# Issuing the store of the first 256 columns of the last token tile from SyncE after the branch join, not from ScalarE inside each branch

## The chip, the cores and the metric

The kernel runs on one core of one Trainium2 chip. The metric is the device time of one execution in microseconds (us); the time before is the median of three runs. A profile of one further execution gives the instruction records, the DMA records and the granted clock.

## What is computed

A transformer-like block on 2048 tokens of width 448, all in float32: an S4 convolution branch and a SwiGLU feed-forward branch, each behind a layer norm that is modulated by a conditioning vector `c`. The reference, cut to its core:

```python
mod = (_silu(c) @ w_mod).reshape(c.shape[0], 6, 1, -1)
sa, ca, ga, sb, cb, gb = (mod[:, k] for k in range(6))
h = _layernorm(x) * (1 + ca) + sa
x = x + ga * _A_ref(h, A_re, A_im, B_re, B_im, C_re, C_im, log_dt, Dskip)   # convolution over the 2048 tokens
h = _layernorm(x) * (1 + cb) + sb
x = x + gb * ((_silu(h @ w_gate) * (h @ w_up)) @ w_down)                     # 448 -> 1792 -> 448
return x
```

## The kernel before

The tokens are cut into 16 tiles of 128 rows (`NT`), a tile being a [128, 448] float32 buffer `xs[i]` in on-chip memory (224 KB), and the tiles into six blocks of 2, 2, 3, 3, 3, 3 (`BLOCKS`, `TILES`). For each block, `ffn` runs over 14 slices of the hidden width (`NF`): `gate_up` (matmuls of line 754, then SiLU on ScalarE, product on VectorE, and a split into a high and a low part) and `down` (matmuls of line 804), while the other engines prepare the next block.

Two versions of this stand in the program, one behind the other: a run-time flag, computed near the start, decides between `small_path` and `general_path` (`tc.If(rv > 0)` and `cond.Else()`, lines 1042 to 1050). The profiled inputs take the first version. At its end every engine jumps over the second version to the join; the profile gives these jumps as COMPARE_BRANCH of line 1042. Behind the join stand only the last stores (lines 1051 to 1053) and the program's closing sequence (the waits for the DMAs and a barrier of all engines, line 1087 in the profile).

The last block (tiles 13, 14 and 15) ends in `finish`. Its matmuls (line 832) leave four sums in four banks: tile 13, tile 14, columns 0 to 255 of tile 15, and columns 256 to 447 of tile 15. VectorE adds each to `xs[i]` (line 843), in this order. Behind the third addition ScalarE issues the store of its 256 columns (line 845), in each version of the program. The stores of tile 13, tile 14 and the last 192 columns of tile 15 are issued by SyncE behind the join (line 1053). SyncE's and ScalarE's DMAs go to two queues, q1 and q10 in the profile; both are served by the core's 16 DMA engines, which also carry the instruction queues q8 and q14. Each engine executes its instructions in order, and so a DMA issue that takes long, or waits, holds back the issues behind it on the same engine. The schedule is written by hand; nothing reorders it.

Of the kernel before, what the change touches and what calls it, by code (L numbers as in the profile page):

```python
# [16 lines left out]
L, D, N, F = 2048, 448, 256, 1792  # L17
NT = L // 128
# [38 lines left out]
def tile_kernel(ctx, tc, x, a_re, a_im, b_re, b_im, c_re, c_im, log_dt,  # L57
                wd, wgate_up, states, groups, vecs, dft, idft, out):
    nc = tc.nc
    sy, ve, sc, po, pe = nc.sync, nc.vector, nc.scalar, nc.gpsimd, nc.tensor  # L60
# [10 lines left out]
    def bank():  # L71
        t = psg.tile([128, 512], F32, name="bank")
        return t

    xs = {}
# [121 lines left out]
    def make_h(h, i, part=None, ca=ca1, sh=sa):  # L197
        m, rs = n1.of[i][0:2]
        if part != 1:
            ve.scalar_tensor_tensor(h, xs[i], m, ca, op0=OP.subtract, op1=OP.mult)  # L200
        if part != 0:
            ve.scalar_tensor_tensor(h, h, rs, sh, op0=OP.mult, op1=OP.add)  # L202
# [527 lines left out]
    def run_blocks(pools, stages, first=None):  # L730
        work, hid = pools.work, pools.hid
        def ffn(ts, fresh, last, todo):
# [89 lines left out]
            def finish():  # L822
                o = [bank(), bank(), CV, DN[0]]
                A, B = slice(0, 256), slice(256, D)
                part = [(0, slice(0, D)), (1, slice(0, D)), (m, A), (m, B)]

                def sums(f, ks):
                    (hi, lo), (wh, wl) = pp[f], wp[f]
                    for k in ks:
                        q, c = part[k]  # L830
                        for z, (u, v) in enumerate(((hi, wh), (hi, wl), (lo, wh))):
                            pe.matmul(o[k][:, c], u[:, q * 128:(q + 1) * 128], v[:, c],
                                      start=f == NF - 2 and z == 0, stop=f == NF - 1 and z == 2)

                sums(NF - 2, (0, 1))
                sums(NF - 1, (0,))
                sums(NF - 2, (2,))
                sums(NF - 1, (1, 2))
                sums(NF - 2, (3,))
                sums(NF - 1, (3,))  # L840
                for k, (q, c) in enumerate(part):
                    i = ts[q]
                    ve.tensor_tensor(xs[i][:, c], o[k][:, c], xs[i][:, c], op=OP.add)  # L843
                    if k == 2:
                        sc.dma_start(out[i * 128:(i + 1) * 128, c], xs[i][:, c])

            for f in range(NF):
                gate_up(f, f + 2 if fresh and f + 2 < NF else None)
# [12 lines left out]
            if last:  # L861
                return finish()
# [144 lines left out]
    def general_path(pools, y):  # L1007
        work = pools.work
        hs = {}

        def s0(i):
            h = h_of(i)
            make_h(h, i)
            t = v0_of(i)
            sy.dma_start(t, y[i * 128:(i + 1) * 128, :])
            po.tensor_tensor(h, h, gd, op=OP.mult)
            po.tensor_tensor(t, t, g0, op=OP.mult)
            hs[i] = h, t

        def s1(i):  # L1020
            h, t = hs.pop(i)
            ve.tensor_tensor(xs[i], h, xs[i], op=OP.add)
            ve.tensor_tensor(xs[i], xs[i], t, op=OP.add)

        def first(i):
            s0(i)
            s1(i)

        return lambda b: (s0, s1), first
# [16 lines left out]
    with cond.Else():  # L1046
        y = general_conv()
        with ExitStack() as es:
            pools = Pools(es)
            run_blocks(pools, *general_path(pools, y))  # L1050
    for i in TILES[-1]:
        c = slice(256 if i + 1 == NT else 0, D)
        sy.dma_start(out[i * 128:(i + 1) * 128, c], xs[i][:, c])


_INS = ["A_u", "A_A_re", "A_A_im", "A_B_re", "A_B_im", "A_C_re", "A_C_im", "A_log_dt", "B_w_down"]
# [29 lines left out]
def build(nc, aps, out):  # L1086
    with tile.TileContext(nc) as tc:
        a = dict(aps)
        tile_kernel(tc, a["A_u"].rearrange("b l d -> (b l) d"), *[a[n] for n in _INS[1:] + ["B_w_gate_up", "A_states", "w_mod_groups", "c_log_dt", "dft", "idft"]],
                    out.rearrange("b l d -> (b l) d"))  # L1090
# [20 lines left out]
```

## Time and profile before

| What | us |
|---|---|
| Median of three runs | 471.81 (471.29 to 472.66) |
| The profiled execution, its device time | 471.9 |
| The profiled execution, span from first to last instruction | 469.8 |
| Last matmul of `finish` starts | 464.7 |
| Last addition of `finish` (line 843) starts | 465.0 |

The granted TensorE clock was 0.999 over the span. A row of the timeline gives the start, the duration, the engine (with a q for its sequencer, which issues DMAs), the line, the operation, and the tiles written and read. A row on one source line gives the number of instructions, then the shortest, the median and the longest duration in ns, and when the first and the last start. "DMA to landing" is the time from the start of an issue to the last part of its data being reported as written. A row on a DMA queue gives its packets, their megabytes, and the time that they took as a share of all 16 DMA engines in that stretch.

### The profile page before, as it was taken

The page shows a single profiled execution, that of the slowest core. Times are in us where ns is not written, and L with a number is a line of the kernel's source. Part 1 is how long each engine was busy: PE and PEld are TensorE (multiplying, and loading weights), DVE is VectorE, ACT ScalarE, POOL GpSimd, SP SyncE. Part 2 cuts the span into 40 slices and gives each one's busy share as a digit, 9 for nine tenths or more (in the row PEclk, how much of TensorE's full clock was granted, in tenths as well). Part 3 has the DMA queues.
Part 4 walks back from the last instruction along what each step waited for, and adds up shares of the span by engine and source line. Part 5 has one row for each costly group of instructions (what it writes and reads, how often), then busy time and mean ns, then how long its engine had stood idle before and what let it go on. Part 6 is the DMA issues. An engine that isn't in the chain of part 4 may idle for free.

```text
span 469.8 us, 7027 instructions
## 1 busy us (share of the span) xinstructions
PE 460.1 (98%) x2735; PEld 438.2 (93%) x2735; DVE 282.6 (60%) x540; ACT 160.1 (34%) x359; POOL 61.6 (13%) x88
## 2 busy tenths in 40 slices
PE   6999999999999999999999999999999999999995
PEld 3669999999999999999999999999999999999995
DVE  4888999778866447573754766464666543222124
ACT  5879666512343222233212223311223222221111
POOL 1122001000000223200022410004141000000000
PEclk9999999999999999999999999999999999999999
DMA  8976653110003000111300011130000112000001
GB/s 303 407 254 179 204 183 102 58 42 2 2 0 100 0 1 0 46 46 46 117 2 0 2 45 46 45 119 1 1 22 24 46 45 80 22 1 1 1 0 65
DMA packets 18779, 31.24 MB, mean 67 GB/s; under 512 B 2608, under 2 KB 13488, under 8 KB 18736
## 3 DMA queue, kind: packets, MB, share of 16 engines
q1 hardware_dynamic: 18096, 30.53, 19.2%
q8 instruction: 23, 0.38, 0.4%
q10 hardware_dynamic: 640, 0.18, 0.2%
q14 instruction: 20, 0.16, 0.1%
HBM read 24.61 MB, written 6.03 MB: 65 GB/s over the span
## 4 chain that ended last, share of the span: by engine, by line
PE 95%; DMA 3%; DVE 1%; SPq 0%; ACT 0%; issue 0%; DVEq 0%
PE bank L754 61%; PE dn L804 28%; DMA wm<-in_w_mod_groups_dram 2%; DMA vec<-in_c_log_dt_dram 1%; PE dn L476 1%; PE bank L256 1%; PE bank L977 1%; PE cv L976 1%; PE cv L978 1%; PE bank L227 0%; SPq L300 0%; DVE x L843 0%; PE bank L394 0%; PE cv L989 0%; PE bank L266 0%; PE bank L269 0%
## 5 line engine op out<-in xcount | busy, mean ns | idle before, releaser
L754 PE MATMUL bank<-hhi,gu 128*128 128x384 f32 (+1 forms) x1176 | 208.9, 317 | 0.2 <-issue 0.2
L754 PEld LDWEIGHTS bank<-hhi,gu 128*128 128x128 f32 x1176 | 189.4, 188 | 3.1 <-issue 1.1
L754 PE MATMUL bank<-hlo,gu 128*128 128x384 f32 (+1 forms) x672 | 130.8, 317 | 0.0
L754 PEld LDWEIGHTS bank<-hlo,gu 128*128 128x128 f32 x672 | 109.1, 188 | 0.2
L784 DVE TENSOR_TENSOR bank<-raw,bank 128x384 f32<-128x384 f32 (+1 forms) x69 | 36.8, 534 | 117.8 <-PE bank L754 115.5
L791 ACT CAST phi<-bank 128x384 fp32r<-128x384 f32 (+1 forms) x83 | 36.8, 444 | 138.9 <-DVE bank L784 138.8
L769 ACT ACTIVATE raw<-bank 128x384 f32<-128x384 f32 (+1 forms) x70 | 32.9, 470 | 119.3 <-PE bank L754 103.7
L792 DVE TENSOR_TENSOR plo<-bank,phi 128x384 fp32r<-128x384 f32 (+1 forms) x83 | 42.5, 511 | 37.6 <-ACT phi L791 37.6
L804 PE MATMUL dn<-wdh,phi 128*128 128x448 f32 x218 | 57.2, 364 | 0.0
L804 PE MATMUL dn<-wdh,plo 128*128 128x448 f32 x218 | 57.1, 362 | 0.0
L804 PE MATMUL dn<-wdl,phi 128*128 128x448 f32 x218 | 56.9, 362 | 0.0
L804 PEld LDWEIGHTS dn<-wdh,plo 128*128 128x128 f32 x218 | 40.9, 187 | 2.7
L804 PEld LDWEIGHTS dn<-wdl,phi 128*128 128x128 f32 x218 | 40.9, 187 | 2.7
L804 PEld LDWEIGHTS dn<-wdh,phi 128*128 128x128 f32 x218 | 38.6, 188 | 1.2
L185 POOL TENSOR_SCALAR rsb<-mvb 128x1 f32<-128x1 f32 (+2 forms) x13 | 4.6, 354 | 142.0 <-DVE mvb L157 142.0
L125 DVE TENSOR_TENSOR gu<-raw,gu 128x1024 fp32r<-128x1024 f32 x14 | 17.1, 1219 | 1.2 <-ACT gu L123 1.2
L185 POOL TENSOR_SCALAR rsa<-mva 128x3 f32<-128x3 f32 (+1 forms) x6 | 2.3, 381 | 98.7 <-DVE mva L157 96.4
L951 POOL TENSOR_TENSOR m<-m,gm 128x448 f32<-128x448 f32 x9 | 10.4, 1155 | 20.8 <-DVE m L202 17.1
L965 DVE TENSOR_TENSOR vl<-m,vh 128x448 fp32r<-128x448 f32 x12 | 9.1, 757 | 6.7 <-ACT vh L964 6.1
L122 ACT CAST gu<-raw 128x768 fp32r<-128x768 f32 x14 | 11.7, 833 | 0.0
L970 POOL TENSOR_TENSOR m<-m,gd 128x448 f32<-128x448 f32 x9 | 11.5, 1280 | 0.0
L215 ACT ACTIVATE raw<-raw,rsb 128x64 f32<-128x64 f32 x14 | 4.8, 345 | 18.9 <-DVE raw L212 9.7
(243 smaller groups left out, 410.2 us busy)
## 6 DMA issues: line engine op xcount, KB each, us to landing
raw<-in_B_w_gate_up_dram SPq DMA_DIRECT2D x14, 512.0 KB, 3.8
rawd<-in_B_w_down_dram SPq DMA_DIRECT2D x16, 224.0 KB, 3.9
x<-in_A_u_dram SPq DMA_DIRECT2D x12, 224.0 KB, 2.9
out_dram<-x SPq DMA_DIRECT2D x11, 224.0 KB, 2.0
xd<-raw SPq DMA_DIRECT2D x9, 256.0 KB, 2.0
raw<-xd SPq DMA_DIRECT2D x36, 64.0 KB, 1.9
wm<-in_w_mod_groups_dram SPq DMA_DIRECT2D x5, 448.0 KB, 8.2
wm<-in_w_mod_groups_dram SPq DMA_DIRECT2D x5, 336.0 KB, 8.2
```

Source lines behind the costliest of these rows:

```text
L122: sc.copy(wgu[j][:, :, 0:3, :], w[:, :, 0:3, :])
L125: ve.tensor_tensor(wgu[j][:, :, 3:7, :], w[:, :, ::-1, :], f32(wgu[j][:, :, 0:4, :][:, :, ::-1, :]), op=OP.subtract)
L185: po.tensor_scalar(rs[:, 0:n], self.mv[:, 0:n, 1], EPS, None, op0=OP.add)
L754: pe.matmul(ps[s][:, 0:n], w[:, s, a], (hlo if lo else hhi)[:, k, first_col(n):first_col(n) + n], start=first and q == 0, stop=end and q = ...
L769: sc.activation(p[:, 0:n], ps[0][:, 0:n], AF.Silu)
L784: ve.tensor_tensor(ps[1][:, 0:n], p[:, 0:n], ps[1][:, 0:n], op=OP.mult)
L791: sc.copy(hi[:, 0:n], ps[1][:, 0:n])
L792: ve.tensor_tensor(lo[:, 0:n], ps[1][:, 0:n], f32(hi[:, 0:n]), op=OP.subtract)
L804: pe.matmul(dn[q][:, 0:D], u[:, cs], v, start=f == 0 and z == 0, stop=f == (NF - 3 if last else NF - 1) and z == 2)
L951: (ve if on_v else po).tensor_tensor(v, h, g, op=OP.mult)
L965: ve.tensor_tensor(vl, v0, f32(vh), op=OP.subtract)
L970: (ve if on_v else po).tensor_tensor(h, h, gd, op=OP.mult)
```

## The change

The issue of ScalarE inside `finish` goes, in both versions. The loop behind the join splits tile 15 into its two column ranges, so that SyncE issues four stores there in place of three. The diff:

```diff
@@ -841,8 +841,6 @@
                 for k, (q, c) in enumerate(part):
                     i = ts[q]
                     ve.tensor_tensor(xs[i][:, c], o[k][:, c], xs[i][:, c], op=OP.add)
-                    if k == 2:
-                        sc.dma_start(out[i * 128:(i + 1) * 128, c], xs[i][:, c])
@@ -1048,9 +1046,10 @@
     for i in TILES[-1]:
-        c = slice(256 if i + 1 == NT else 0, D)
-        sy.dma_start(out[i * 128:(i + 1) * 128, c], xs[i][:, c])
+        for c in (slice(0, 256), slice(256, D)) if i + 1 == NT else (slice(0, D),):
+            sy.dma_start(out[i * 128:(i + 1) * 128, c], xs[i][:, c])
```

SyncE's instructions at the end of the program, before (-) and with the change (+). `x_73`, `x_74` and `x_75` are the buffers of tiles 13, 14 and 15; what is waited for stands in brackets, DMAHW being the semaphore of an earlier DMA:

```order
 L811 DMA rawd_83<-in_B_w_down_dram 128x448 [waits DMAHW6_49,DVE_49]
-L1042 UNCONDITIONAL_BRANCH
-L1053 DMA out_dram<-x_73 128x448 [waits DMAHW2_49,DVE_49]
-L1053 DMA out_dram<-x_74 128x448 [waits DMAHW3_49,DVE_49]
-L1053 DMA out_dram<-x_75 128x192 [waits DMAHW4_49,DVE_49]
-L1087 UNCONDITIONAL_BRANCH
+L1040 UNCONDITIONAL_BRANCH
+L1052 DMA out_dram<-x_73 128x448 [waits DMAHW1_49,DVE_49]
+L1052 DMA out_dram<-x_74 128x448 [waits DMAHW2_49,DVE_49]
+L1052 DMA out_dram<-x_75 128x256 [waits DMAHW3_49,DVE_49]
+L1052 DMA out_dram<-x_75 128x192 [waits DMAHW4_49,DVE_49]
+L1086 UNCONDITIONAL_BRANCH
```

The store of 256 columns now stands between the store of tile 14 and the store of the last 192 columns, in SyncE's order and on SyncE's queue.

ScalarE's instructions at the end of the program (the lines of the changed kernel are two lower from here on):

```order
 L769 ACTIVATE raw<-bank 128x384 [waits PE_49,Activation_49]
 L778 CAST phi<-bank 128x128 [waits DVE_49] x3
-L845 DMA out_dram<-x_75 128x256 [waits DVE_49]
-L1042 UNCONDITIONAL_BRANCH
-L1087 UNCONDITIONAL_BRANCH
+L1040 UNCONDITIONAL_BRANCH
+L1086 UNCONDITIONAL_BRANCH
```

ScalarE's jump to the join now stands right behind its last cast. The instructions of TensorE, VectorE and GpSimd are the same as before, in the same order.

## The prediction

> **What bounds the kernel now.** I read the page first, then the timeline of the end, then the rows of the store lines, then the DMA queues in short stretches.
>
> ```profile
> span 469.8 us, 7027 instructions
> PE 460.1 (98%) x2735; PEld 438.2 (93%) x2735; DVE 282.6 (60%) x540; ACT 160.1 (34%) x359; POOL 61.6 (13%) x88
> PE 95%; DMA 3%; DVE 1%; SPq 0%; ACT 0%; issue 0%; DVEq 0%
> ```
>
> TensorE is busy 98% of the span and 95% of the chain of waits. Its instructions do not change. What can move is the end, when TensorE is done:
>
> ```profile
> 462.87 0.27 ACT L778 CAST phi<-bank 128x128 fp32r<-128x128 f32 x1 [0.69 <-DVE bank L777]
> ...
> 463.57 1.15 DVE L843 TENSOR_TENSOR x<-bank,x 128x448 f32<-128x448 f32 x2
> ...
> 464.21 2.80 SPq L1053 DMA_DIRECT2D out_dram<-x  x3
> ...
> 464.63 0.42 DVE L843 TENSOR_TENSOR x<-cv,x 128x256 f32<-128x256 f32 x1
> ...
> 465.03 0.36 DVE L843 TENSOR_TENSOR x<-dn,x 128x192 f32<-128x192 f32 x1
> 465.08 0.36 ACTq L845 DMA_DIRECT2D out_dram<-x  x1
> ```
>
> All results are in on-chip memory at 465.39 (465.03 + 0.36), yet the span ends at 469.8. These 4.4 us are stores and closing sequence. The second and the third of SyncE's stores and ScalarE's, one by one:
>
> ```profile
> L1053 SPq DMA_DIRECT2D out_dram<-x x1: 1249/1249/1249, 464.7 to 464.7; - x1
> ...
> DMA to landing us min/median/max: 3.7/3.7/3.7
> ...
> L1053 SPq DMA_DIRECT2D out_dram<-x x1: 931/931/931, 466.1 to 466.1; - x1
> ...
> DMA to landing us min/median/max: 2.6/2.6/2.6
> ...
> L845 ACTq DMA_DIRECT2D out_dram<-x x1: 363/363/363, 465.1 to 465.1; - x1
> ...
> DMA to landing us min/median/max: 2.8/2.8/2.8
> ```
>
> Tile 14's issue takes 1.25 us, that of the last 192 columns (not begun until tile 14's is over, though its data were ready at 465.4) 0.93. The landings are at 464.75 + 3.7 = 468.4, 466.1 + 2.6 = 468.7 and, for ScalarE's, 465.08 + 2.8 = 467.9. The store of the last 192 columns lands last, and the end follows 469.8 - 468.7 = 1.1 us behind it. What the change is worth is how far that landing moves.
>
> A store issue need not take so long. Three stores with 0.84 us between them, in an earlier block:
>
> ```profile
> L867 SPq DMA_DIRECT2D out_dram<-x x3: 333/356/357, 306.8 to 309.2; - x3
> ...
> DMA to landing us min/median/max: 1.9/2.0/2.2
> ```
>
> So the two issues at the end are held up by 0.9 and 0.6 us. The queues show by what:
>
> ```profile
> q8 instruction: 1, 0.02, 6.6%
> ...
> q10 hardware_dynamic: 126, 0.11, 45.2%
> q14 instruction: 2, 0.02, 10.1%
> q1 hardware_dynamic: 10, 0.01, 6.9%
> ...
> q8 instruction: 1, 0.02, 5.5%
> ```
>
> The first row is for 464 to 465: one instruction packet, which starts at 464.6 and takes 6.6% of 16 engines for 1 us, that is 1.05 us of one engine. The middle three are for 465.75 to 466.5: SyncE's queue (q1) moves 10 packets, left-overs of tile 13, while ScalarE's (q10) moves 126. Tile 14's data are not yet moving, since SyncE's issue hangs until 466.0. ScalarE's store passed it. In the same stretch two more instruction packets lie on single engines. The last row (467.25 to 468.3) is a further one, 0.92 us. My reading: while one DMA engine carries an instruction packet, SyncE's queue takes one more DMA and holds the next issue until that engine is free. Two rows from earlier speak for it:
>
> ```profile
> L86 SPq DMA_DIRECT2D x<-in_A_u_dram x1: 1393/1393/1393, 92.9 to 92.9; - x1
> ...
> q8 instruction: 1, 0.02, 125.8%
> ```
>
> The load at 92.9, issued behind others, took 1.39 us; the instruction packet beside it starts in the stretch 92.90 to 92.95 and takes 125.8% of 16 engines for 0.05 us, 1.0 us.
>
> Where the packets come from: each engine jumps to the join and must have new instructions.
>
> ```profile
> L1042 PEldq COMPARE_BRANCH x1: 3430/3430/3430, 463.7 to 463.7; - x1
> L1042 DVEq COMPARE_BRANCH x1: 51/51/51, 465.0 to 465.0; - x1
> L1042 ACTq COMPARE_BRANCH x1: 43/43/43, 465.5 to 465.5; - x1
> ...
> L1087 ACTq DRAIN x1: 81/81/81, 468.1 to 468.1; - x1
> L1087 DVEq DRAIN x1: 59/59/59, 468.3 to 468.3; - x1
> L1087 SPq DRAIN x1: 7/7/7, 469.0 to 469.0; - x1
> ```
>
> TensorE's jump takes 3.43 us; VectorE is back 3.3 us after its jump, ScalarE 2.6. The Trainium skill, "Runtime: NRT & Kernel Launch", section "Instruction fetch mechanics", says that a taken branch whose target is outside the current window forces a DMA fetch before execution goes on. The trace agrees, with packets about 1 us behind the jumps; the page's 16 KiB blocks fit q8 (one packet, 0.02 MB) but not q14, whose two packets share 0.02 MB.
>
> **The change part by part.**
>
> *Removed.* ScalarE's issue (0.36 us) and a store that never lands last: nothing on the path. ScalarE's jump moves from 465.5 to right behind its last cast, 463.1 (462.87 + 0.27). Its instruction packet moves as much, to about 464, ahead of all stores: one of the two q14 packets leaves the stretch in which the stores run. Between nothing and the 0.6 us by which the third issue is held up now may be saved by it.
>
> *Unchanged.* Tile 13 at 464.21; tile 14 from 464.75 to 466.0, since TensorE's jump and its packet stay. TensorE's and VectorE's code is the same.
>
> *Added.* A fourth issue on SyncE, at 466.1, where that of the last 192 columns stands now. Bounds: 0.33 us (shortest row of line 867) to 1.25 us (tile 14's). I take 0.93, what the issue at this instant, behind the same two stores and beside VectorE's packet, takes now: it is the nearest row. It ends at 467.0. Behind it, with 0.1 us between issues (466.1 - 466.0), the last 192 columns start at 467.1 in place of 466.1. Their own issue then takes 0.36 (line 867) in place of 0.93, since the packets of VectorE and ScalarE are past, and ends at 467.5 in place of 467.0: 0.5 us later. The landing came 468.7 - 467.0 = 1.7 us behind the end of the issue; undisturbed it is 2.0 - 0.36 = 1.6. So 469.1 to 469.2, **0.4 to 0.5 us later**. TensorE's second packet (0.92 us of one engine, from 467.8) can hold a sixteenth of these data:
>
> ```profile
> 464.50:465.00 0.50, 0.49 (x5) 0.32 (x3) 0.50 (x2) 0.00 (x0) 0.00 (x0) 1.00 0.13 33
> 465.00:465.25 0.25, 0.00 (x0) 0.00 (x0) 0.25 (x2) 0.00 (x0) 0.00 (x0) 1.00 0.65 244
> ```
>
> The last two columns are the DMA share and GB/s. Tile 13's data begin about 465.05, 0.5 us behind the end of its issue (464.21 + 0.34). So the last columns' data would begin at 468.0, and the held engine is free at 468.7. This is up to 0.2 us more, and I count it in the range.
>
> *Elsewhere.* Both versions lose one ScalarE instruction; no wait, buffer or order before 463 changes. The cost is nothing, and no cover is needed for it.
>
> Sum: 0 + 0 + 0.45. Against the profiled execution 471.9 + 0.45 = 472.35; against the median, which lies 0.1 lower, 472.3. The bounds: with both new issues short, -0.7 (below); with both held, +1.9 (below).
>
> **The rivals.**
>
> *A. Only the bytes count.* The four stores are the same 672 KB on the same 16 engines, whoever issues them, if no issue is held up. At 466.5 there remain 448 KB (224 + 128 + 96), 0.46 MB.
>
> ```profile
> 91.91 0.92 SPq L86 DMA_DIRECT2D rawd<-in_A_u_dram  x2
> ...
> 466.50:466.75 0.25, 0.00 (x0) 0.00 (x0) 0.00 (x0) 0.00 (x0) 0.00 (x0) 1.00 0.81 307
> ...
> 467.25:467.50 0.25, 0.00 (x0) 0.00 (x0) 0.00 (x0) 0.00 (x0) 0.00 (x0) 1.00 0.18 63
> ```
>
> Two issues that follow each other freely take 0.46 us each (first row), so the last would end at 466.1 + 0.92 = 467.0, as now. At the 307 GB/s of the second row the bytes take 1.5 us, until 468.0, with 0.4 us to the landing (now the last data move at 468.3 and land at 468.7): 468.4, 0.3 us earlier than now, so 471.5. For it: with ScalarE's packet gone, the issue at 466.1 may be short. Against it: the engines stand almost idle in the third row because the next issue was late, so issues do count today. The floor of this case is VectorE's return at 468.3: the last drain of SyncE, at 469.0, can come forward to that at most, 0.7 us, 471.1. The Trainium skill, "DMA: Bandwidth & Descriptors", section "Issuing engines are not separate DMA queues", speaks for this rival: all issuers' DMAs run on the same 16 engines, and issuing on several saves only sequencer time. The trace differs in one point: ScalarE's store flowed while SyncE's was held.
>
> *B. Slower beyond doubt: a third hold-up.* The issue of the 256 columns takes tile 14's 1.25 us, until 467.35, and the next one, from 467.45, is still at work when TensorE's second packet starts (467.8). It is then held until that packet ends, 467.8 + 0.92 = 468.7, plus the 0.3 us that tile 14's issue stays behind its packet (464.6 + 1.05 = 465.7, end 466.0): 469.0. Landing 1.6 behind, 470.6, against 468.7: +1.9 us, and +1.6 if it is released at the packet's very end. I put it between, at 473.5. It decides where the fourth issue has not ended by 467.8. Against it: line 867's issues into an idle queue were short each time, and from 467.25 to 467.5 the queues are nearly empty.
>
> *C. Something outside the end*, by the shifted ScalarE code: no row speaks for it; TensorE is busy 98% up to there whatever the other engines fetch.
>
> **How the numbers follow.** About 0.3% (1.4 us) is what a measurement of this kernel can tell from no change; the three runs spread over 1.4 us. Forecast (+0.45): 0.48, of which 0.05 would be measured over +0.3%. Rival A: 0.29, of which 0.03 under -0.3%. Rival B: 0.17, of which 0.12 over +0.3%. C: 0.06, half each way. Faster 0.03 + 0.03 = 0.06; slower 0.05 + 0.12 + 0.03 = 0.20; within 0.74. The forecast's own range is 471.8 to 472.8; from A's 471.5 less 0.4 of spread up to the lower part of B gives 471.1 to 473.4.
>
> **What would show it.** In the changed profile: tile 14's issue still about 1.25 us; the issue of the 256 columns at 466.1 near 0.9 (A: near 0.4; B: over 1.2); the last issue at 467.1, near 0.4; the last landing at 469.1; ScalarE's drain at about 466 in place of 468.1, and TensorE's jump still 3.4 us. A time outside 471.1 to 473.4 with the same code on TensorE would mean that the end isn't what moved, and the reading of the hold-ups falls if tile 14's issue is short although the packet at 464.6 is there.

## The result, and the profile after

The changed kernel takes 472.9 us in the median of 22 runs (471.24 to 473.8), the kernel before 471.6 beside it: a ratio of 1.0026, 95% interval 1.0019 to 1.0033, or 1.2 us slower (0.9 to 1.6). That is within the 0.3% that the prediction called no change (the upper end of the interval, 0.33%, just passes it), but clear of zero. The times are not spread around one value: three of the 22 runs lie between 471.24 and 471.45, the other nineteen from 472.38 on.

The end of the profiled execution (span 471.9 us), from its timeline:

```profile
463.07 0.27 ACT L778 CAST phi<-bank 128x128 fp32r<-128x128 f32 x1 [0.69 <-DVE bank L777]
...
464.42 3.18 SPq L1052 DMA_DIRECT2D out_dram<-x  x4
...
465.23 0.36 DVE L843 TENSOR_TENSOR x<-dn,x 128x192 f32<-128x192 f32 x1
```

All four stores are SyncE's now. This execution comes to its end 0.2 us later than that of the kernel before (first store at 464.42, before 464.21); I count from the first store's issue where I compare. The last three issues, from the rows of the store line:

```profile
L1052 SPq DMA_DIRECT2D out_dram<-x x1: 1432/1432/1432, 464.9 to 464.9; - x1
...
L1052 SPq DMA_DIRECT2D out_dram<-x x1: 631/631/631, 466.5 to 466.5; - x1
...
DMA to landing us min/median/max: 2.0/2.0/2.0
...
L1052 SPq DMA_DIRECT2D out_dram<-x x1: 400/400/400, 467.2 to 467.2; - x1
...
DMA to landing us min/median/max: 3.6/3.6/3.6
```

Tile 14's issue is held as before, the issue of the 256 columns hardly (0.63), the last one is free (0.40). But the last store lands 3.6 us behind its issue, at 470.8, where the store before it needed 2.0. SyncE waits for it:

```profile
SPq L1087 <- DMA out_dram<-x: 1.5, 3, 0.8
...
SPq L1086 <- DMA out_dram<-x: 3.0, 3, 2.3
```

The first row is the kernel before, the second the changed one; each gives the total in us, the number of waits and the longest. One wait in the closing sequence takes 2.3 us; the longest of this kind was 0.8 before. The DMA queues show what happens, in three stretches (468.20 to 468.25, 468.6 to 469.6, and 469.6 to 470.4):

```profile
q8 instruction: 1, 0.02, 179.4%
q1 hardware_dynamic: 22, 0.02, 102.0%
...
DMA packets 1, 0.01 MB, mean 8 GB/s; under 512 B 0, under 2 KB 0, under 8 KB 0
...
DMA packets 9, 0.01 MB, mean 8 GB/s; under 512 B 1, under 2 KB 9, under 8 KB 9
...
q1 hardware_dynamic: 9, 0.01, 5.8%
```

At 468.2 an instruction packet on q8 begins in the middle of the last store's data. The profile doesn't name the owner of a packet; I take this one for TensorE's second, since it comes 0.6 us behind TensorE's return at 467.6 and since q8's packets move with TensorE's jump in f2. Its size: 179.4% of 16 engines for 0.05 us is 1.44 us of one engine, until 469.66. For a whole microsecond no data of the store move (the one packet of the second stretch is another instruction packet). Then nine packets of SyncE's queue follow, eight of a row each and one small one: a sixteenth of 128 rows and its report, what one DMA engine has to do for this store. So 15 of 16 parts were done before 468.6, and the one behind the instruction packet made the kernel wait.

ScalarE is back at 465.7, and TensorE's jump took 3.62 us. ScalarE's earlier jump did not clear the stretch of the stores, though. From 465.9 to 466.8 there are again two packets on q14, as there were before:

```profile
q14 instruction: 2, 0.02, 5.8%
```

One of them starts 0.6 us behind ScalarE's return, as TensorE's second does behind TensorE's; that it is a second packet of ScalarE's is my reading, since the profile doesn't name its owner.

### The profile page after: what moved, and what is told of

Same layout as the page of the kernel before. It is cut to its first block, busy times and chain, and to the rows that moved or that the text cites. A ratio compares the mean times of both kernels' runs of the same rounds, so it can differ in the third digit from the quotient of the medians.

```text
span 471.9 us, 7028 instructions
## 1 busy us (share of the span) xinstructions
PE 461.5 (98%) x2735; PEld 439.4 (93%) x2735; DVE 282.7 (60%) x540; ACT 159.8 (34%) x359; POOL 61.5 (13%) x88
## 4 chain that ended last, share of the span: by engine, by line
PE 94%; DMA 3%; DVE 1%; SPq 0%; ACT 0%; issue 0%; DVEq 0%
PE bank L754 60%; PE dn L804 28%; DMA wm<-in_w_mod_groups_dram 2%; DMA vec<-in_c_log_dt_dram 1%; PE dn L476 1%; PE bank L256 1%; PE bank L975 1%; PE cv L976 1%; PE cv L974 1%; PE bank L227 0%; DVE x L843 0%; PE cv L987 0%; PE bank L394 0%; PE bank L266 0%; SPq L300 0%; PE bank L269 0%
```

## The experiments

**The packet theory**: what is lost is the last store's share on the one DMA engine that carries TensorE's second instruction packet. It is lost when that engine's rows of the store are not past when the packet starts. **The issue theory**, the rival: four issues one behind the other on SyncE are slower than three on SyncE and one on ScalarE, whatever the packets. Ratios are against the kernel before, run beside each.

**e1: four matmuls more on TensorE behind the last.**

```diff
                 sums(NF - 1, (3,))
+                for _ in range(4):
+                    pe.matmul(DN[1][:, 0:D], pp[NF - 1][0][:, 0:128], wp[NF - 1][0], start=True, stop=True)
```

> The changed kernel with four more 448-column matmuls on TensorE behind the last of finish, into a bank that nobody reads: nothing else changes, and TensorE's jump to the join comes about 0.8 us later. Packet theory (the loss is the share of the last store on the one DMA engine that carries TensorE's second instruction packet): that packet starts at about 469.0 in place of 468.2, behind the last store's data; the last landing is at 468.8 to 469.0 in place of 470.8, and the kernel gets FASTER than the changed one by some 1 us in the median (0 to +0.4 us against before) although it does more work. Issue theory (the loss is that SyncE issues four stores one behind the other): no gain, +1.2 us against before as the changed kernel, or more.

Measured: 473.9 us, 1.0038 (1.0025 to 1.0051), +1.8 us. The jump did not move as intended.

```profile
L1042 PEldq COMPARE_BRANCH x1: 3546/3546/3546, 464.1 to 464.1; - x1
...
q8 instruction: 1, 0.02, 180.2%
...
DMA packets 9, 0.01 MB, mean 6 GB/s; under 512 B 1, under 2 KB 9, under 8 KB 9
```

The jump is at 464.1, in an execution whose first store is 0.1 us later than in the changed kernel's, so it came about 0.05 us later and not 0.8. The second packet starts between 468.30 and 468.35, and the same nine packets are late (stretch 469.6 to 470.6). The jump starts ahead of the matmuls that stand before it: the four new ones run from 465.13 to 466.12. So matmuls that wait for nothing do not hold TensorE's sequencer back here; f2 shows a wait that does. The run does not tell the theories apart; it repeats the loss.

**e2: five stores.**

```diff
-        for c in (slice(0, 256), slice(256, D)) if i + 1 == NT else (slice(0, D),):
+        for c in (slice(0, 256), slice(256, 352), slice(352, D)) if i + 1 == NT else (slice(0, D),):
```

> The changed kernel with the last 192 columns stored in two parts of 96, five issues on SyncE in place of four. Packet theory: the rows that are held leave when the packet ends (469.7), whether in one store or two: last landing 470.8 to 471.1, +1.3 to +1.6 us against before. Issue theory: every issue on SyncE costs 0.5 to 0.7 us at the end, so +1.8 to +2.0 us against before.

Measured: 474.35 us, 1.0047 (1.0034 to 1.006), +2.2 us with an interval of 1.6 to 2.8: over what the packet theory expected, and nearer to the issue theory's 1.8 to 2.0.

```profile
L1052 SPq DMA_DIRECT2D out_dram<-x x5: 338/441/1628, 464.6 to 468.0; - x5
...
q8 instruction: 1, 0.02, 169.4%
...
DMA packets 18, 0.01 MB, mean 9 GB/s; under 512 B 18, under 2 KB 18, under 8 KB 18
```

In the profile the packet theory's picture stands: twice nine packets, of both small stores, come behind the instruction packet (470.0 to 470.7). But tile 14's issue was held 1.63 us here, so everything behind it is later, and all five runs lie above 473.6: by their times, no execution got its data past the packet. By its time alone the run is inconclusive.

**e3: tile 15 in one store by SyncE.**

```diff
-        for c in (slice(0, 256), slice(256, D)) if i + 1 == NT else (slice(0, D),):
+        for c in (slice(0, D),):
```

> The changed kernel with tile 15 stored whole, three issues on SyncE and none on ScalarE. The last store is issued at about 466.5 in place of 467.2, its data move from 467.5 to 468.2. Packet theory: nearly all of them are past when TensorE's second packet starts at 468.2; last landing about 468.7, 0 to +0.3 us against before; where a few rows are caught in the profile they land at 470 to 470.8. Issue theory: one issue less than the changed kernel, one fewer step of 0.5 to 0.7 us: +0.5 to +0.7 us against before.

Measured: 472.07 us, 1.0008 (0.9999 to 1.0017), +0.4 us with an interval of 0 to 0.8. The twelve runs lie from 471.34 to 473.53. The last store begins earlier, at 465.9, 2.1 us behind the first (in the changed kernel 2.8); the packet starts in 467.80 to 467.95 beside the last few rows and reports:

```profile
L1052 SPq DMA_DIRECT2D out_dram<-x x3: 337/728/1473, 463.8 to 465.9; - x3
...
q8 instruction: 1, 0.02, 36.6%
q1 hardware_dynamic: 15, 0.01, 13.5%
```

Nothing was late in this execution (span 469.5). By the time both theories remain, since the measured interval covers what either expected.

**e4: the two parts of tile 15 exchanged.** SyncE stores the 256 columns, ScalarE the last 192, inside each version.

```diff
+                    if k == 3:
+                        sc.dma_start(out[i * 128:(i + 1) * 128, c], xs[i][:, c])
...
-        for c in (slice(0, 256), slice(256, D)) if i + 1 == NT else (slice(0, D),):
+        for c in (slice(0, 256) if i + 1 == NT else slice(0, D),):
```

> ScalarE issues the store of the last 192 columns inside each version (behind the fourth addition), SyncE those of tile 13, tile 14 and the 256 columns. Packet theory: ScalarE's store is past by 467, SyncE's third is issued at 466.1 to 466.5 and moves before 468; last landing at 468.5 to 468.7, -0.3 to +0.1 us against before. Issue theory: three issues on SyncE as before: 0.

Measured: 472.13 us, 1.0000 (0.9992 to 1.0009), as both expected. Its profile shows how a packet holds an issue:

```profile
L1054 SPq DMA_DIRECT2D out_dram<-x x3: 337/338/1326, 465.1 to 466.1; - x3
...
q8 instruction: 1, 0.02, 110.2%
```

TensorE's first packet came late in this execution, at 466.10 (the stretch 466.10 to 466.15), 1.0 us behind the first store's issue, where it was 0.4 before. Tile 14's issue, past by then, took 0.34 us, and the next one, which began at 466.1, was held 1.33. One point of the expectation failed: ScalarE's store was not past by 467, but was issued at 466.3 and landed 3.1 us later. The run was the slowest of its eleven (472.78).

**f1: the changed kernel once more, as the control.**

> The changed kernel once more, as the control for the two kernels beside it. Both theories: +0.9 to +1.6 us against before. Packet theory: a profile in which the 16th part of the last landing comes some 2 us behind the 15th, or, if this execution is one of the few that the first series had near 471.3 us, with it.

Measured: 473.24 us, 1.0024 (1.0007 to 1.004), +1.1 us as expected, with a wide interval (0.3 to 1.9). Five of its twelve runs lie from 471.37 to 472.03, the other seven from 473.16 to 475.48. The profiled one was the quickest, 471.37, span 469.5:

```profile
L1052 SPq DMA_DIRECT2D out_dram<-x x4: 338/438/1517, 464.0 to 466.7; - x4
...
DMA to landing us min/median/max: 1.7/2.6/3.3
...
q8 instruction: 1, 0.02, 114.4%
q1 hardware_dynamic: 12, 0.00, 33.8%
...
SPq L1086 <- DMA out_dram<-x: 1.0, 3, 0.5
```

This is the run that decides most, since the program is the same. Four issues on SyncE, tile 14's held 1.52 us, the last at 466.7: 2.7 us behind the first, as in the slower profile (2.8). The second packet starts at 467.96, when only a few rows and reports of the store are left. The last store lands 1.7 us behind its issue, at 468.4, 4.4 behind the first issue; in the slower profile it is 6.4, and in the kernel before 4.5 (468.7 - 464.2). Four issues alone thus cost nothing here. What differs is 0.1 us in the last issue (2.7 against 2.8 behind the first) and 0.2 us in the packet (4.0 against 3.8).

That the store's data are still moving when the packet starts is not enough. In the kernel before, too, it starts among them, at 467.85 (the rows are for 467.8 to 467.9), and nothing is late:

```profile
q8 instruction: 1, 0.02, 57.9%
q1 hardware_dynamic: 29, 0.02, 55.6%
```

The traces have the rows of the last store by their 768 bytes. The packet starts 0.12 us behind the first of them in the changed kernel's profile and 0.20 in e1's, where eight rows were held, and 0.33 to 0.34 in the kernel before and in the control, where none was. One such row takes 0.036 us in the median, so an engine with nothing else to do has its eight past in about 0.3 us (an estimate, 8 times 0.036). This fits the theory; it rests on four profiles, and none names the engine that a packet or a row is on.

**f2: TensorE's jump waits for the last addition.**

```diff
                     ve.tensor_tensor(xs[i][:, c], o[k][:, c], xs[i][:, c], op=OP.add)
+                pe.matmul(DN[1][:, 0:8], xs[ts[m]][:, 256:384], xs[ts[m]][:, 440:D], start=True, stop=True)
```

> The changed kernel with one 8-column matmul on TensorE that reads what VectorE's last addition writes, so that TensorE's sequencer waits for that addition before it jumps (four matmuls without a wait left the jump nearly where it was, since the sequencer runs ahead of the array). The jump comes at about 465.7 in place of 463.9, its first instruction packet at 466.6 in place of 464.8, the second at about 470 in place of 468.2. Packet theory: tile 14's issue is not held (0.34 to 0.45 us in place of 1.43), the last issue begins before 466.6, its data are past long before the second packet, and the last landing is at 468.0 to 468.6; the end is then set by TensorE's return at 469.3, so 0 to +0.5 us against before, some 1 us FASTER than the control. Issue theory: four issues on SyncE as in the control, +0.9 to +1.6 us.

Measured: 472.58 us, 1.0016 (1.0008 to 1.0025): +0.8 us, over the 0 to +0.5 of the packet theory, quicker than the control by less than I expected, and the intervals overlap. By its time the run does not tell the theories apart.

```profile
L1041 PEldq COMPARE_BRANCH x1: 4410/4410/4410, 465.2 to 465.2; - x1
...
463.97 1.86 SPq L1053 DMA_DIRECT2D out_dram<-x  x4
...
L1053 SPq DMA_DIRECT2D out_dram<-x x4: 338/370/407, 464.0 to 465.4; - x4
...
q8 instruction: 1, 0.02, 231.8%
...
DMA to landing us min/median/max: 4.1/4.1/4.1
```

With the jump moved from 463.9 to 465.2, no issue is held: four of them take 1.86 us with the waits between. That half was as expected. The other half was not: the first packet, at 466.18, now lies in the data of the two last stores and takes 1.85 us of one engine (231.8% of 16 for 0.05 us), so the last store lands 4.1 us behind its issue, at 469.5. Moving the jump moved the hold from the issues to the data. It also left little to win: the jump took 4.41 us, so TensorE was back only at 469.6, and the closing barrier of all engines could not have come much sooner.

**f3: tile 15 by ScalarE behind the join.**

```diff
-        for c in (slice(0, 256), slice(256, D)) if i + 1 == NT else (slice(0, D),):
-            sy.dma_start(out[i * 128:(i + 1) * 128, c], xs[i][:, c])
+        (sc if i + 1 == NT else sy).dma_start(out[i * 128:(i + 1) * 128, :], xs[i])
```

> Tile 15 stored whole by ScalarE behind the join, tiles 13 and 14 by SyncE: ScalarE jumps at 463.1 and is back at 465.7, so it issues at 465.7 to 466.1 on its own queue. Packet theory: its data move at 466.6 to 467.3, beside tile 14's, and are past before TensorE's second packet (468.2); last landing 468.0 to 468.4, span 469.2 to 469.6: -0.6 to -0.1 us against before. Issue theory: two issues on SyncE in place of three, -0.5 us or more.

Measured: 471.76 us, 0.9994 (0.9985 to 1.0003), the same as before within -0.7 to +0.1 us, with none of the twelve runs above 472.31. Both theories had a time in that interval, so it does not decide between them. ScalarE, back from its jump, issues at 465.74:

```profile
464.32 2.00 SPq L1051 DMA_DIRECT2D out_dram<-x  x2
465.74 0.36 ACTq L1051 DMA_DIRECT2D out_dram<-x  x1
```

Tile 14's held issue does not hold ScalarE's queue. The end is now tile 14's landing, 3.9 us behind its issue at 464.85.

**g1: the two versions in the other order.** The version that runs here stands second, so that all engines run straight into the join, and jump at the start instead.

```diff
-    with tc.If(rv > 0) as cond:
+    with tc.If(rv < 1) as cond:
+        y = general_conv()
         with ExitStack() as es:
             pools = Pools(es)
-            run_blocks(pools, small_path(pools))
+            run_blocks(pools, *general_path(pools, y))
     with cond.Else():
-        y = general_conv()
+        xs.update({i: xbuf[i % 4] for i in range(4)})
         with ExitStack() as es:
             pools = Pools(es)
-            run_blocks(pools, *general_path(pools, y))
+            run_blocks(pools, small_path(pools))
```

> The changed kernel with its two versions in the other order (the general one first, the one that runs here second), so that every engine runs straight from the end of the version into the join and jumps at the start instead. Packet theory: no instruction packet is fetched for a jump near the stores; SyncE's four issues take 0.33 to 0.45 us each, and the last landing comes 3.0 to 3.5 us behind the start of the first store's issue, in place of 6.4 (profile of the changed kernel) or 4.4 (its second profile); runs spread little. The whole time says less, since the jump now costs up to 3.5 us at the start: between -2 and +3 us against before. Issue theory: four issues one behind the other stay as costly as in the changed kernel, landing 4.4 us or more behind the first issue.

Measured: 475.2 us, 1.0076 (1.0063 to 1.009), +3.6 us (3.0 to 4.2): more than the -2 to +3 that I allowed. TensorE's jump at the start takes 3.71 us in place of 0.09, and the first store comes 4.2 us later than before (468.4 against 464.2); what the other 0.6 us are is not shown. From the first store's issue to the end of the span it is 4.3 us, in the kernel before 5.6. At the end:

```profile
L1053 SPq DMA_DIRECT2D out_dram<-x x4: 343/370/407, 468.4 to 469.8; - x4
...
DMA to landing us min/median/max: 1.8/2.0/2.1
...
DMA packets 576, 0.69 MB, mean 86 GB/s; under 512 B 64, under 2 KB 576, under 8 KB 576
```

The last row is for 466 to 474: only the 576 packets of the four stores, and no instruction packet. All issues are free, and the last landing is 3.2 us behind the first issue (469.83 + 1.8 - 468.4).

**g2: the kernel before in that order**, ScalarE storing the 256 columns.

> The kernel before with its two versions in the other order: ScalarE stores the 256 columns as before. Beside the same order with SyncE issuing all four. Packet theory: with no packets near the stores, who issues the store of 256 columns is worth the time of one free issue at most, so the two are 0 to 0.5 us apart. Issue theory: 0.9 to 1.6 us apart, as the changed kernel and the one before.

Measured: 475.81 us, 1.0076 (1.0062 to 1.009), the same ratio as g1's; with five runs each, the two intervals leave room for about 0.9 us either way.

```profile
L1055 SPq DMA_DIRECT2D out_dram<-x x3: 332/344/344, 469.8 to 471.0; - x3
...
DMA to landing us min/median/max: 2.0/2.0/2.0
```

The last landing is again 3.2 us behind the first issue (471.0 + 2.0 - 469.8), and the span ends 4.3 to 4.4 us behind it in both (472.7 - 468.4 in g1, 474.2 - 469.8 here). The profiles decide here more than the times: with no instruction packet near the stores, who issues the fourth store is worth nothing that these runs show. The issue theory, which wanted 0.9 to 1.6 us between g1 and g2 whatever the packets, falls.

## Why the prediction was right, and which size was off

*The forecast*, no change by 0.3%, with +0.45 us: the measured +1.2 us lies inside the range and inside that bound, but outside the forecast's own range (472.9 against 471.8 to 472.8). That it was right on no change is in part luck: the delay of the issues, from which the +0.45 was added up, came to nothing (-0.1 in the control's profile, below), and the loss came from a term that the sum left out. The wide range held 472.9 because it reached up to rival B.

*The fourth issue at 0.93 us* was too dear: 0.63 and 0.46 in the two profiles. Rival A had expected a short issue here, with ScalarE's packet gone from the stretch; but there are two q14 packets in it after the change as before, so the *Removed* part had that wrong. What is gone is ScalarE's store, which moved 126 packets there. Whether this made the issue shorter is not shown, since no run took the one away without the other.

*The last issue ends 0.5 us later*: 0.3 to 0.4 later (3.1 to 3.2 us behind the first issue in the two profiles; 467.0 - 464.2 = 2.8 before).

*The landing 1.6 to 1.7 us behind the end of the last issue*: 468.4 - (466.7 + 0.41) = 1.3 in the control's profile. With no packet near it is 1.8 - 0.41 = 1.4 (g1). With this the sum of the issues comes to -0.1 and not +0.45.

*TensorE's second packet, "up to 0.2 us more", counted in the range*: this is the term that was mis-sized. I had seen that it could hold a sixteenth of the data, but took the packet at the 0.92 us it needed in the profile before. It took 1.4 us in the changed kernel's profile and in e1's, and the held rows then needed about another microsecond to move and to be reported (from 469.66 to 470.8). Together this is 2.0 us (6.4 against 4.4 behind the first issue), or nothing. By their times, 19 of the 22 executions of the first series and 7 of the 12 of the second lost some of it, and this share would set the median; only one execution of each kind was profiled.

*Rival A*, only the bytes count, comes near what an execution does that gets past the packet: span 469.5 against 469.8, 0.3 us as it said, though the spread of either kernel is wider than that. *Rival B* had nearly the price of the other case (+1.6 to +1.9 us), but by a third held issue; the third issue took 0.63 us and the fourth 0.40, and the data were held. *Rival C*: nothing was seen outside the end. *Holding of issues by a packet*: right in each run that moved or removed the packet (e4: 1.33 us on the next issue; f2 and g1: none held).

*ScalarE back at about 466*: 465.7.

## What to carry to other kernels

In this kernel a jump at the end of the program puts instruction packets beside the last stores. Each of TensorE's took 0.9 to 1.85 us of one DMA engine, which was enough to hold the next issue on a queue or a sixteenth of a store. So look for such packets beside the last stores. Two queues keep a held issue from holding the other engine's (f3: ScalarE's issue took 0.36 us while SyncE's hung), though no run here was clearly faster than the kernel before. And where a kernel's times fall into two groups, profile it twice: the same program, once in each group, tells more than a variant.

## What was not expected of the hardware

One instruction packet on q8 took from 0.9 us to 1.85 us of a DMA engine. The longest (f2: 231.8% of 16 engines for 0.05 us) had stores flowing beside it, but so had one of 0.88 us (e4: 110.2% for 0.05 us); what makes the difference stays open. A jump over the other version took TensorE 3.4 to 3.9 us, at either end of the program, and 4.4 in f2, while matmuls placed ahead of it that wait for nothing hardly delayed it (e1: about 0.05 us for four).
